# Two o matmuls moved by one place each in an attention and FFN kernel that TensorE bounds

## The chip, the cores and the metric

One core of a Trainium2 chip. The metric is the device time of one execution in microseconds (us), as a median over several executions; lower is better. Ratios are the mean time of one kernel's runs over that of the other's runs of the same rounds, so they are not quite the ratio of the medians that stand beside them. "Trace" is the profiler's record of one execution.

## The reference, cut to what matters

```python
B, H, S, Nb, D = 8, 8, 576, 16, 64
k_all = concat([beacon_k, k], axis=2); v_all = concat([beacon_v, v], axis=2)
scores = q @ k_all.T / sqrt(D)             # causal over the 576 keys, the 16 beacons always seen
a = softmax(scores); attn = a @ v_all
x = attn.transpose(0, 2, 1, 3).reshape(B * S, H * D)          # 4608 x 512
out = (gelu(x @ w_gate) * (x @ w_val)) @ w_out                # 512 -> 1536 -> 512
```

Eight batches of attention, then a gated FFN over all 4608 tokens. The kernel works in bf16 with float32 sums.

## The kernel before

The FFN works on chunks of 512 tokens, and each chunk's last product (the "o matmuls") is kept back: it is issued, a few matmuls at a time, inside the attention of the next batch, to fill TensorE while ScalarE computes exps. One step of the outer loop is thus: attention of batch b with 48 o matmuls of chunk b-1 strewn in (from batch 2 on, the first 12 are each split into two of 64 rows), then 96 gate and value matmuls ("gv").

Some words used below. A "burst" is a run of score matmuls, which read 64 rows each. "Values" is the product of the exps with v, by "head" or by "pair" of heads; it reads up to 128 rows. A "mode turn" is the place where TensorE goes from matmuls of 64 rows to matmuls of 128 or back. A "slot" is one of the three buffers of psum_s, where a burst's scores stay until ScalarE has computed their exps. "From start to start" is the time from the first matmul of a group to the first matmul of the next.

The helpers that matter (cut):

```python
psum_s = pool(name="psum_s", bufs=3, PSUM)   # 3 slots of two banks: scores, values pairs, gv
psum_t = pool(name="psum_t", bufs=1, PSUM)   # one bank
psum_o = pool(name="psum_o", bufs=1, PSUM)   # one bank

def scores(b, *parts):         # score matmuls on 64 rows, then one exp by ScalarE frees the slot
    s_ps = psum_s.tile(...)
    ...score matmuls of parts into s_ps...
    act(exp_ring[...], s_ps[...], ACT.Exp, scale=QK_SCALE)
    if b:
        ...masks(b, m, c): GpSimd affine_select on the diagonal blocks...

def av_head(b, m, hi, pool, tag):   # values of one head: 15 matmuls, then normalize (VectorE)
    x = pool.tile([P, 1, 512], FP32)
    attend(b, m, hi, x[:, 0, :])
    normalize(b, m, x, hi, hi + 1)  # reciprocal, then y_sb = x * r: frees the bank

def av(b, m):                       # both heads of a pair: 30 matmuls, in a psum_s slot
def out_mms(ci, u0, u1):            # o matmuls; every 12th starts a new bank, psum_t or psum_o
```

The stretch that the change touches, once for each of batches 1 to 7:

```python
            o(5 if b == 1 else 6)
            av_head(b, 0, 0, psum_t, "t")
            o(1)
            scores(b, (1, 1))           # third burst: three parts, 14 matmuls (10 in batch 1)
            scores(b, (2, 0))
            scores(b, (2, 2))
            ahead(2)                    # two loads for batch 2, in batch 1 alone
            av_head(b, 0, 1, psum_t, "t")
            turn_dma(b, 0)
            o(7)
            scores(b, (2, 1))           # fourth burst, 18 matmuls
            scores(b, (2, 3), (3, 3))
            scores(b, (3, 0))           # reuses the slot of (2, 2): waits for its exp
            av_head(b, 1, 0, psum_o, "o")
            o(5)
            av_head(b, 1, 1, psum_o, "o")
            turn_dma(b, 1)
            scores(b, (3, 1))
            scores(b, (3, 2))
            av(b, 2)                    # values pair 2
            turn_dma(b, 2)
            o(6)
            av(b, 3)                    # values pair 3: needs the masks of (3, 2)
            turn_dma(b, 3)
            o(11)
            ...gv matmuls of chunk b...
```

The softmax here doesn't subtract the row's maximum and nothing guards it: scores larger than these inputs give would overflow.

## Time and profile before

| | before |
|---|---|
| median of all 6 runs made beside the changed kernel | 365.87 us (365.26 to 366.03) |
| span of the traced execution | 363.7 us |
| TensorE busy | 98% of the span |
| attention stretch of batches 2 to 6, first o matmul to first gv matmul | 18.12 us each |
| the same of batch 1 and batch 7 | 19.11 and 18.17 us |

The kernel is one long chain on TensorE. In such a kernel the summed views (busy shares, waits) say only that little is left.

### The profile page before, as it was taken

The numbers are of one execution on the slowest core, as the hardware profiler recorded it, in microseconds if no ns is written. First come the engines' busy times: TensorE is split into PE (matmuls) and PEld (weight loads), VectorE is DVE, ScalarE is ACT, GpSimd is POOL, SyncE is SP. The second block draws the span as 40 slices with busy tenths as digits, with TensorE's granted clock in tenths as the row PEclk, the third lists the DMA queues.
The fourth block names the chain that finished last, engine by engine and source line by source line (L and its number), as shares of the span: only waits on it lengthen the run. The fifth ranks groups of instructions, "written<-read, shape, count | busy, mean of one in ns | idle before, by whom it ended". The sixth has DMA issues, their size and how long they took to land.

```text
span 363.7 us, 7774 instructions
## 1 busy us (share of the span) xinstructions
PE 356.0 (98%) x3206; PEld 186.8 (51%) x3206; DVE 163.0 (45%) x320; ACT 193.2 (53%) x252; POOL 161.2 (44%) x288
## 2 busy tenths in 40 slices
PE   7899999999999999999999999999999999999996
PEld 6665446444654455445644564446544564444443
DVE  4547846343543345434534354334443453333322
ACT  3965787238923693358633891379335953321210
POOL 8934397656536552845384645565320530000000
PEclk9999999999999999999999999999999999999999
DMA  8999999899179956999299917992795132000112
GB/s 105 175 203 204 197 125 109 122 175 182 28 122 146 214 46 83 155 212 69 56 151 213 116 38 124 171 192 30 116 139 128 17 68 108 0 2 29 58 38 108
DMA packets 160419, 41.57 MB, mean 114 GB/s; under 512 B 146944, under 2 KB 155904, under 8 KB 160384
## 3 DMA queue, kind: packets, MB, share of 16 engines
q0 software_dynamic: 104848, 19.11, 68.9%
q1 hardware_dynamic: 55536, 21.96, 30.3%
q8 instruction: 25, 0.41, 0.5%
q14 instruction: 10, 0.08, 0.1%
HBM read 38.27 MB, written 9.44 MB: 131 GB/s over the span
## 4 chain that ended last, share of the span: by engine, by line
PE 96%; DVE 3%; issue 0%; ACT 0%
PE gv_ps L168 45%; PE o_ps L168 26%; PE x_ps L168 9%; PE s_ps L168 6%; PE v_ps L168 3%; PE g_ps L168 3%; PE t_ps L176 2%; DVE qkT L235 1%; DVE o_sb L481 1%; PE w_ps L168 1%; PE y_ps L176 0%; ACT qkT L171 0%; DVE y_sb L356 0%; DVE o_sb L479 0%; DVE qkT L239 0%
## 5 line engine op out<-in xcount | busy, mean ns | idle before, releaser
L171 ACT ACTIVATE ge_sb<-gv_ps 128x512 bf16<-128x512 f32 x95 | 55.9, 597 | 135.3 <-PE gv_ps L168 134.1
L433 DVE TENSOR_TENSOR hT_sb<-gv_ps,ge_sb 128x512 bf16<-128x512 f32 x95 | 64.9, 691 | 105.4 <-ACT ge_sb L171 105.3
L171 ACT ACTIVATE expT<-s_ps 128x992 bf16<-128x992 f32 (+3 forms) x112 | 100.7, 974 | 11.3 <-PE s_ps L168 10.3
L168 PE MATMUL o_ps<-wo_sb,hT_sb 128*128 128x512 bf16 (+3 forms) x516 | 104.7, 373 | 0.9 <-DVE o_sb L481 0.9
L168 PE MATMUL gv_ps<-xT_sb,wg_sb 128*128 128x512 bf16 x380 | 105.4, 379 | 0.0
L168 PE MATMUL gv_ps<-xT_sb,wv_sb 128*128 128x512 bf16 x380 | 105.3, 379 | 0.0
L320 POOL TENSOR_SCALAR_AFFINE_SELECT expT<-expT 128x256 bf16<-128x256 bf16 (+1 forms) x140 | 52.3, 391 | 49.4 <-ACT expT L171 48.0
L168 PEld LDWEIGHTS <-wv_sb 128*128 128x128 bf16 x432 | 42.3, 98 | 50.6
L168 PEld LDWEIGHTS <-wg_sb 128*128 128x128 bf16 x432 | 42.1, 98 | 49.9
L168 PEld LDWEIGHTS <-hT_sb 128*128 128x128 bf16 (+1 forms) x516 | 40.8, 96 | 42.5 <-issue 4.1
L168 PEld LDWEIGHTS <-expT 128*128 128x128 bf16 (+1 forms) x960 | 33.6, 97 | 9.9 <-DVE y_sb L356 3.1
L168 PE MATMUL x_ps<-v_sb,expT 128*128 128x65 bf16 (+1 forms) x960 | 37.5, 193 | 0.1
L111 POOL DMA_DIRECT2D v_sb<-in_v_dram x40 | 33.6, 858 | 5.9 <-DMA wv_sb<-in_moe_w_val_dram 1.7
L168 PE MATMUL s_ps<-qkT 64*128 64x80 bf16 (+5 forms) x528 | 33.2, 250 | 2.4 <-DVE qkT L239 1.4
L111 POOL DMA_DIRECT2D k_sb<-in_k_dram x30 | 25.2, 844 | 16.7 <-DMA v_sb<-in_v_dram 8.2
L111 POOL DMA_DIRECT2D q_sb<-in_q_dram x30 | 25.3, 874 | 10.2 <-DMA wo_sb<-in_moe_w_out_dram 3.6
L356 DVE TENSOR_TENSOR y_sb<-x_ps,r_sb 128x320 bf16<-128x320 f32 (+1 forms) x47 | 28.8, 612 | 1.8 <-DVE r_sb L354 0.2
L479 DVE COPY o_sb<-o_ps 128x512 f32<-128x512 f32 (+2 forms) x31 | 20.7, 668 | 15.1 <-PE o_ps L168 14.2
L354 DVE RECIPROCAL r_sb<-x_ps 128x5 f32<-128x5 f32 (+1 forms) x47 | 9.6, 204 | 38.4 <-PE x_ps L168 38.4
L168 PEld LDWEIGHTS <-qkT 64*128 64x128 bf16 x528 | 18.7, 95 | 15.2 <-issue 7.0
L399 POOL COPY hold_sb<-xT_sb 128x2 bf16<-128x2 bf16 x6 | 1.1, 186 | 31.2 <-DMA xT_sb<-y_sb 31.2
L433 DVE TENSOR_TENSOR hT_sb<-v_ps,ge_sb 128x512 bf16<-128x512 f32 x13 | 9.0, 692 | 9.5 <-PE v_ps L168 9.5
(58 smaller groups left out, 151.6 us busy)
## 6 DMA issues: line engine op xcount, KB each, us to landing
out_dram<-o_sb SPq DMA_DIRECT2D x35, 256.0 KB, 7.2
v_sb<-in_v_dram POOLq DMA_DIRECT2D x24, 128.0 KB, 9.5
q_sb<-in_q_dram POOLq DMA_DIRECT2D x18, 128.0 KB, 12.6
k_sb<-in_k_dram POOLq DMA_DIRECT2D x18, 128.0 KB, 5.7
wo_sb<-in_moe_w_out_dram POOLq DMA_DIRECT2D x3, 512.0 KB, 14.4
wg_sb<-in_moe_w_gate_dram POOLq DMA_DIRECT2D x2, 512.0 KB, 11.3
wv_sb<-in_moe_w_val_dram POOLq DMA_DIRECT2D x2, 512.0 KB, 12.8
v_sb<-in_v_dram POOLq DMA_DIRECT2D x8, 112.0 KB, 5.7
```

The source lines that it names most:

```text
L111: keep(nc.gpsimd.dma_start(out=out_ap, in_=in_ap))
L168: keep(nc.tensor.matmul(out_ap, lhsT, rhs, start=start, stop=stop, **kw))
L171: keep(nc.scalar.activation(out_ap, in_ap, func, **kw))
L176: keep(nc.tensor.transpose(out_ap, in_ap, ident[0:n, 0:n]))
L235: keep(nc.vector.tensor_copy(out_ap, in_ap))
L320: nc.gpsimd.affine_select(out=d, in_=d, pattern=[[0, 2], [1, n]], compare_op=ALU.is_ge, fill=0.0, base=0, channel_multiplier=-1,)
L354: keep(nc.vector.reciprocal(r, x[:, :, :, D:DV]))
L356: nc.vector.tensor_tensor(out=y_of[i][:, :, h0:h1, :].rearrange("p j b d -> p b j d"), in0=x[:, :, :, 0:D], in1=r.to_broadcast([P, h1 - h0 ...
L399: keep(nc.gpsimd.tensor_copy(hold_sb, x[:, 0 : S : S - 1]))
L433: keep(nc.vector.tensor_tensor(out=h_of[ci][:, fi, :], in0=v_ps, in1=ge_sb, op=ALU.mult))
L479: keep(nc.vector.tensor_copy(o_ap, o_ps))
L481: keep(nc.vector.tensor_copy(o_ap, o_half))
```

## The change

Its intent, as the order tells it: start the exps of the third burst sooner, and give the last values pair more cover for its masks. No instruction is added or taken away, and only TensorE's order differs.

```diff
             av_head(b, 0, 0, psum_t, "t")
-            o(1)
             scores(b, (1, 1))
             scores(b, (2, 0))
             scores(b, (2, 2))
             ahead(2)
+            o(1)
             av_head(b, 0, 1, psum_t, "t")
 ...
             av(b, 2)
             turn_dma(b, 2)
-            o(6)
+            o(7)
             av(b, 3)
             turn_dma(b, 3)
-            o(11)
+            o(10)
```

Below, "part 1" is the first hunk and "part 2" the second.

## The prediction

> **What bounds the kernel now.** I read the page first (shares of the engines, then the chain that ended last), then who waited for whom, then the matmul timeline of single batches, because the change touches only a stretch of some 14 us in each of the seven later batches.
>
> ```profile
> PE 356.0 (98%) x3206; PEld 186.8 (51%) x3206; DVE 163.0 (45%) x320; ACT 193.2 (53%) x252; POOL 161.2 (44%) x288
> ...
> PE 96%; DVE 3%; issue 0%; ACT 0%
> ```
>
> TensorE (PE) is busy 98% of the span and makes up 96% of the chain that ended last. The other engines are half idle on average. No matmul is added or removed, so only bubbles between matmuls can be won. The three waits at issue, in sums over the whole run:
>
> ```profile
> ACT expT L171 <- PE s_ps L168: 10.3, 23, 1.0
> PEld L168 <- DVE y_sb L356: 4.6, 21, 0.3
> PEld L168 <- POOL expT L320: 0.8, 4, 0.2
> ```
>
> The first costs nothing directly (ScalarE is not the bound); the other two stop a weight load, and so TensorE. Most of the 4.6 us are not a full wait, as shown below. So the room is well under 2% of 365 us (7.3 us) before any detail.
>
> The detail: batch 3 between 128 and 142 us. First the third score burst (14 score matmuls), all engines, then the fourth burst and the last two values pairs on TensorE, and the same fourth burst in batch 7.
>
> ```profile
> 130.40 0.38 PE L168 MATMUL o_ps<-wo_sb,hT_sb 128*128 128x512 bf16 x1
> 130.71 0.81 PE L168 MATMUL s_ps<-qkT 64*128 64x80 bf16 x14
> 130.83 0.49 DVE L356 TENSOR_TENSOR y_sb<-x_ps,r_sb 128x320 bf16<-128x320 f32 x1
> 131.21 1.00 ACT L171 ACTIVATE expT<-s_ps 128x992 bf16<-128x992 f32 x1 [0.44 <-PE s_ps L168]
> 131.45 0.42 PE L168 MATMUL x_ps<-v_sb,expT 128*128 128x65 bf16 x8
> ```
>
> The o matmul starts at 130.40 and the scores at 130.71: 0.31 us, where a 512-column matmul in a stream takes 0.216 (eleven o matmuls took 2.37). So 0.10 us is a bubble at the turn from 128-row to 64-row matmuls; there is another of 0.09 at the turn back to x_ps. The exp of the burst waits 0.44 us for its scores. The second head (131.45) follows the normalize of the first (y_sb, done 131.32) by 0.13, so y_sb is just in time.
>
> ```profile
> 133.52 0.87 PE L168 MATMUL s_ps<-qkT 64*128 64x80 bf16 x18
> 134.33 0.62 PE L168 MATMUL x_ps<-v_sb,expT 128*128 128x65 bf16 x15
> ...
> 136.94 1.08 PE L168 MATMUL x_ps<-v_sb,expT 128*128 128x65 bf16 x30
> 137.87 1.46 PE L168 MATMUL o_ps<-wo_sb,hT_sb 128*128 128x512 bf16 x6
> 139.16 1.14 PE L168 MATMUL x_ps<-v_sb,expT 128*128 128x65 bf16 x30
> 140.14 2.54 PE L168 MATMUL o_ps<-wo_sb,hT_sb 128*128 128x512 bf16 x11
> ```
> ```profile
> 289.40 0.79 PE L168 MATMUL s_ps<-qkT 64*128 64x80 bf16 x18
> 290.13 0.63 PE L168 MATMUL x_ps<-v_sb,expT 128*128 128x65 bf16 x15
> ```
>
> From start to start, the fourth burst takes 0.81 us in batch 3 and 0.73 in batch 7. Inside the trace the difference is one gap of 69 ns, in batches 2 to 6, before its last score part: that part reuses the PSUM slot whose exp, the last of the third burst, ends at 133.95. In batch 7 TensorE happened to arrive later and did not wait. The same values work (30 matmuls) takes 0.93 us for pair 2 and 0.98 for pair 3: a gap of 57 to 58 ns behind the first matmul of pair 3, where its second weight load waits for the last mask of GpSimd (138.81 to 139.22).
>
> **What the Trainium skill says.** "TensorEngine Tiling (Array Packing)", Key Properties, says that a change of tiling mode drains TensorE. The trace agrees and prices it: 94 to 104 ns at each turn between 64-row scores and 128-row work, and none between x_ps and o_ps, which have 128 rows both. "Perfetto Trace Analysis", Optimization Strategy, advises to look for gaps on the limiting engine and for the semaphore behind each; that is the method here. "TensorE: Matmul & The Clock Gate", Back-to-back issue gap, gives N/2.4 + 2.5 ns, 216 ns for 512 columns, where sustained it quotes 131; this trace has 216 in long streams, so I use 0.216 us.
>
> **The change part by part.** The changed program, compared in the order of its instructions, differs on TensorE alone; the other four engines run the same list.
>
> Part 1, in batches 1 to 7: x(head 0), o, scores, x(head 1) becomes x, scores, o, x. Mode turns before: o to scores, scores to x. After: x to scores, scores to o. Two each, at 97 + 94 ns before and 100 + 94 after (x to scores takes 99 to 102 elsewhere in the batch): nothing, +3 ns. Head 1 begins at the same time, as the same work lies ahead of it. What moves is the scores: 0.31 - 0.10 = 0.21 us earlier. Then the exp starts 0.21 us earlier, since it had been idle for 0.44 us, and the two exps that follow it back to back also end 0.21 us earlier, the last at 133.74 in place of 133.95. The fourth burst then finds its slot free (it would need it at 133.93): the 69 ns go, in five batches (2 to 6): 5 x 0.069 = 0.35 us. In batch 7 there is none to win; its 0.14 us wait for a late y_sb ahead of head 1 stays, for VectorE's list is the same and the o matmul that moves was inside that wait's shadow before as after.
>
> Does the earlier burst meet a wait of its own? Its last part needs the exp that ends at 130.76 (batch 3). It would start at 131.16 - 0.22 = 130.94: free, by 0.13 us with the semaphore's 0.04. Batch 7 likewise. In batch 1 not: there ScalarE is behind, and the exp ends at 53.13 while the part would start at 52.99. It loses 0.20 us there:
>
> ```profile
> 52.18 0.95 ACT L171 ACTIVATE expT<-s_ps 128x928 bf16<-128x928 f32 x1
> ...
> 52.76 0.80 PE L168 MATMUL s_ps<-qkT 64*128 64x80 bf16 x10
> ...
> 58.92 1.30 PE L168 MATMUL x_ps<-v_sb,expT 128*128 128x65 bf16 x30
> 60.06 1.46 PE L168 MATMUL o_ps<-wo_sb,hT_sb 128*128 128x512 bf16 x6
> ```
>
> But pair 2 of batch 1 takes 1.14 us where it takes 0.93 in batch 3: it waits 0.205 us for masks that GpSimd does late, between its own DMA issues. A delay of 0.20 is swallowed there. Batch 1 comes out at 0, give or take 0.1.
>
> Part 2, in batches 1 to 7: one o matmul moves from behind the last pair to ahead of it. 0.216 us of work now lies where 58 ns were lost, so the mask is in time. Batches 2 to 7: 6 x 0.058 = 0.35 us; batch 1 shows no such gap. The transposing DMA of the last pair leaves 0.216 - 0.058 - 0.07 = 0.09 us later, while the FFN of the chunk starts 0.127 earlier. It takes 2.6 us to land after its issue at 141.70, so 144.3; the first matmul that reads it is the thirteenth of the FFN stream, 142.52 + 12 x 0.216 = 145.1. The 0.8 us of slack shrink to 0.6: no new wait.
>
> Sum: 0.35 + 0.35 + 0 = 0.70 us less, 0.19%. 365.3 - 0.7 = 364.6 us.
>
> **The rivals.** (a) The burst waits in more batches than the first: it is 0.13 us from doing so, and a wait there is a loss of TensorE with the o matmul stuck behind it in order. If all of 2 to 7 lost 0.1 us, 0.6 us would go and the result would be 365.2. Against it: the exps of batches 2 to 7 lie within 0.02 us of each other in the trace. (b) Batch 1's 0.20 us isn't swallowed, because with ScalarE later the masks come later too: 364.8. (c) y_sb turns into the bound ahead of head 1: it is done 0.08 us before it is needed, and it does not move; but a weight load that could run under the o matmul is held up a little: at most 0.02 us x 7. (d) ScalarE's lead is worth more than I count and removes gaps elsewhere: I found no other gap that is not a mode turn or TensorE's own y_sb wait, so at most 0.3 us more. (e) Nothing happens, because the gaps only move on to the FFN: there the gv stream shows no gap after the first matmul, so what is won before it is kept.
>
> **Range and chances.** The terms are small against the runs' scatter: the three of before go from 365.26 to 365.93. I take 364.6 with 363.9 to 365.4: below, d and scatter; above, a plus b. 2% would be 7.3 us, ten times all that I can find, and no dependence changes that could cost that much: faster 0.01, same 0.98, slower 0.01.
>
> **What would show it.** Fourth burst of batches 2 to 6 at 0.74 us from start to start; pair 3 at 0.92 to 0.93 in all batches; ScalarE's wait ahead of the third burst's exp down from 0.44 to about 0.22; third burst of batch 1 longer by 0.2 and its pair 2 shorter by as much; head 1 starting as long after head 0 as now; no gap in the FFN streams. It is wrong if the third burst waits for exps in batches 2 to 7, if pair 3 still has its gap, or if the span does not fall by the sum of the closed gaps.

## The result, and the profile after

The changed kernel takes 364.71 us (median of 6, 364.54 to 365.37) where the kernel before takes 365.87 (median of 6, 365.26 to 366.03). The ratio is 0.9975, with a 95% interval from 0.9963 to 0.9988: 0.25% faster, clear of noise and inside the 2% that counts as the same. The predicted 364.6 us is 0.1 off; how much of that is luck is told below.

The page of the changed kernel, its engines:

```profile
PE 353.7 (97%) x3164; PEld 187.5 (52%) x3206; DVE 163.4 (45%) x320; ACT 193.0 (53%) x252; POOL 161.3 (44%) x288
```

The 2.3 us that TensorE seems to have lost are no gain. 42 of 3206 matmul records are missing from this trace (the weight loads are all there): 24 o matmuls and 18 gv matmuls. The traces of the first four experiments lack 42 too; the other six traces lack none. In the stretches below, the o matmul that is missing is the first behind a values group: from start to start such a values group has some 0.22 us in it that belong to an o matmul not shown, and the next o group has a count one too small. This is to be kept in mind in the timelines.

TensorE in batch 3 of the changed kernel (columns: start in us, length in us, engine, line, operation, out<-in, shape, count):

```profile
130.29 0.62 PE L168 MATMUL x_ps<-v_sb,expT 128*128 128x65 bf16 x15
130.84 0.80 PE L168 MATMUL s_ps<-qkT 64*128 64x80 bf16 x14
131.58 0.39 PE L168 MATMUL o_ps<-wo_sb,hT_sb 128*128 128x512 bf16 x1
131.81 0.61 PE L168 MATMUL x_ps<-v_sb,expT 128*128 128x65 bf16 x15
...
133.87 0.79 PE L168 MATMUL s_ps<-qkT 64*128 64x80 bf16 x18
134.59 0.62 PE L168 MATMUL x_ps<-v_sb,expT 128*128 128x65 bf16 x15
...
139.64 1.07 PE L168 MATMUL x_ps<-v_sb,expT 128*128 128x65 bf16 x30
140.55 2.32 PE L168 MATMUL o_ps<-wo_sb,hT_sb 128*128 128x512 bf16 x10
```

ScalarE's exp behind the third burst there:

```profile
131.34 1.00 ACT L171 ACTIVATE expT<-s_ps 128x992 bf16<-128x992 f32 x1 [0.22 <-PE s_ps L168]
```

From head 0 (130.29) to head 1 (131.81) it is 1.52 us, as before (129.94 to 131.45, 1.51). The exp waits 0.22 us in place of 0.44. The fourth burst takes 0.72 us from start to start in place of 0.81, and pair 3 takes 0.91 in place of 0.98 (its missing record lies behind pair 2 here, so this group is whole).

Batch 6 of the changed kernel shows what the prediction had not seen:

```profile
247.19 0.97 PE L168 MATMUL s_ps<-qkT 64*128 64x80 bf16 x14
248.09 0.39 PE L168 MATMUL o_ps<-wo_sb,hT_sb 128*128 128x512 bf16 x1
```

Here the third burst takes 0.91 us from start to start, in batch 3 only 0.74. The table has the attention stretch of each batch, from the start of its first o matmul to the start of its first gv matmul, in us, read from the matmul starts of each trace. Between these stretches the FFN is the same to 1 ns. So the difference of two kernels is known from single traces to some 10 ns in batches 2 to 5 and some 20 ns in batches 6 and 7 (batch 7 has 18.105 to 18.126 us in the four traces that have both parts there and no padding), which the medians of the times can't give: they carry the start of the program, which took from 21.3 to 23.6 us up to the first FFN matmul in the eleven traces.

| batch | before | after | part 1 alone | part 2 alone | fourth burst later | after, padded |
|---|---|---|---|---|---|---|
| 1 | 19.106 | 19.104 | 19.118 | 19.120 | 19.191 | 19.471 |
| 2 | 18.122 | 17.969 | 18.032 | 18.056 | 18.033 | 17.963 |
| 3 | 18.120 | 17.962 | 18.027 | 18.049 | 18.033 | 17.961 |
| 4 | 18.121 | 17.966 | 18.029 | 18.054 | 18.037 | 17.967 |
| 5 | 18.120 | 17.965 | 18.033 | 18.049 | 18.031 | 17.968 |
| 6 | 18.121 | 18.137 | 18.195 | 18.053 | 18.037 | 17.965 |
| 7 | 18.174 | 18.109 | 18.172 | 18.121 | 18.171 | 17.964 |
| sum less before | | -0.672 | -0.278 | -0.382 | -0.351 | -0.625 |

The sum after is -0.67 us where -0.70 was predicted. But it is made of four batches with -0.15 to -0.16, one with +0.02 (batch 6), one with -0.065 and one with nothing. The two traced spans hardly differ (363.7 and 363.6 us), because the changed kernel's traced execution began its first FFN matmul 0.50 us later (22.38 against 21.88); its fastest runs have a span of 362.8.

### The profile page after: what moved, and what is told of

Its sections match the earlier page's. It is cut to its first block, busy times and chain, and to the rows that moved or that the text cites. A ratio compares the mean times of both kernels' runs of the same rounds, so it can differ in the third digit from the quotient of the medians.

```text
span 363.6 us, 7732 instructions
## 1 busy us (share of the span) xinstructions
PE 353.7 (97%) x3164; PEld 187.5 (52%) x3206; DVE 163.4 (45%) x320; ACT 193.0 (53%) x252; POOL 161.3 (44%) x288
## 4 chain that ended last, share of the span: by engine, by line
PE 88%; DMA 5%; DVE 3%; POOL 2%; issue 1%; ACT 0%; SPq 0%; POOLq 0%
PE gv_ps L168 40%; PE o_ps L168 25%; PE x_ps L168 9%; PE s_ps L168 6%; DMA q_sb<-in_q_dram 3%; PE v_ps L168 3%; PE g_ps L168 3%; PE t_ps L176 2%; DMA k_sb<-in_k_dram 1%; DVE qkT L235 1%; POOL v_sb L111 1%; PE w_ps L168 1%; DVE o_sb L481 1%; DMA xT_sb<-y_sb 1%; POOL k_sb L111 0%
## 5 line engine op out<-in xcount | busy, mean ns | idle before, releaser
L168 PE MATMUL o_ps<-wo_sb,hT_sb 128*128 128x512 bf16 (+3 forms) x492 | 101.0, 373 | 2.3 <-DVE o_sb L481 0.9
L168 PE MATMUL gv_ps<-xT_sb,wv_sb 128*128 128x512 bf16 x364 | 101.7, 379 | 0.4
```

The source lines that it names most:

```text
L168: keep(nc.tensor.matmul(out_ap, lhsT, rhs, start=start, stop=stop, **kw))
```

## The experiments

All outputs are right. The first four ran in one call, on one chip, with 11 runs of the kernel before (median 365.66 us; two of them took 368.0 and 368.3, so these intervals are wide); the next four in another (365.92 us); the last as one look. Each was timed with six runs, the last with one.

**Part 1 alone.** Is the gain of the fourth burst due to the earlier exp, and what does the early burst cost?

```diff
 (the first hunk of the change; the last pair as before)
```

> Part 1 alone (third burst right behind the first head), last pair as before. My theory: the fourth burst of batches 2 to 6 falls from 0.805 us to 0.72 (its slot wait goes), pair 3 keeps its 0.98, the third burst is held for 0.17 us in batch 6 and 0.2 in batch 1 (swallowed by pair 2 there). By attention stretch against before: batches 2 to 5 about -0.09 us each, 6 about +0.08, 7 and 1 about 0; in all -0.3 us. Rival (the whole gain is part 2's, the fourth burst gets shorter only because all before it moved): fourth burst stays at 0.805, total 0.

Measured: 365.47 us, ratio 0.9977 (0.9948 to 1.0007), too wide for the times to tell. TensorE in batch 3:

```profile
133.97 0.79 PE L168 MATMUL s_ps<-qkT 64*128 64x80 bf16 x18
134.69 0.62 PE L168 MATMUL x_ps<-v_sb,expT 128*128 128x65 bf16 x15
...
139.52 1.14 PE L168 MATMUL x_ps<-v_sb,expT 128*128 128x65 bf16 x30
140.50 2.54 PE L168 MATMUL o_ps<-wo_sb,hT_sb 128*128 128x512 bf16 x11
```

The fourth burst is at 0.72, pair 3 keeps its 0.98. The stretches fell by 0.09 us in batches 2 to 5, and batch 6 grew by 0.07, as my theory had it. The rival (all of it is part 2's) falls: part 2 was not in this kernel.

**Part 2 alone.** The wait of the last pair.

```diff
 (the second hunk of the change; the single o matmul ahead of the third burst as before)
```

> Part 2 alone (one more o matmul ahead of the last values pair). My theory: pair 3 falls from 0.98 to 0.912 us in batches 2 to 7, fourth burst stays at 0.805, third burst as before: 6 x -0.068 = -0.4 us. Rival (the mask comes later by as much, the wait only moves): pair 3 stays at 0.98, total 0.

Measured: 365.35 us, ratio 0.9982 (0.9951 to 1.0012). In batch 3:

```profile
135.19 0.87 PE L168 MATMUL s_ps<-qkT 64*128 64x80 bf16 x18
135.99 0.62 PE L168 MATMUL x_ps<-v_sb,expT 128*128 128x65 bf16 x15
...
141.04 1.07 PE L168 MATMUL x_ps<-v_sb,expT 128*128 128x65 bf16 x30
141.95 2.32 PE L168 MATMUL o_ps<-wo_sb,hT_sb 128*128 128x512 bf16 x10
```

Now it is the other way round: the fourth burst stays at 0.80, pair 3 falls to 0.91. Six batches lose 0.053 to 0.071 us each. The two parts together, -0.278 and -0.382, make -0.660, and the whole change has -0.672: they add up, and neither feeds the other.

**Fourth burst later.** If its gap is a wait for the slot that the last exp of the third burst frees, more time must close it as well as an earlier exp does.

```diff
             turn_dma(b, 0)
-            o(7)
+            o(8)
             scores(b, (2, 1))
 ...
             turn_dma(b, 3)
-            o(11)
+            o(10)
```

> Before, with one o matmul moved from the end of the stretch to ahead of the fourth burst; third burst and last pair untouched. If the 83 ns of the fourth burst are a wait for the PSUM slot that the third burst's last exp frees, giving it 0.216 us more time closes them without any earlier exp: fourth burst 0.72 us in batches 2 to 6, in all -0.4 us, and the third burst of batch 6 not held. If the gap has another cause (order of parts, a bank), it stays at 0.805 and the total is 0.

Measured: 365.36 us, ratio 0.9974 (0.9942 to 1.0006). In batch 3:

```profile
134.01 0.79 PE L168 MATMUL s_ps<-qkT 64*128 64x80 bf16 x18
134.74 0.62 PE L168 MATMUL x_ps<-v_sb,expT 128*128 128x65 bf16 x15
```

The burst takes 0.72 us with the third burst where it was, and 0.084 to 0.089 us go in batches 2 to 6, batch 6 among them, whose third burst is not held. So what the gap needs is time, as a wait for that slot would, and not an earlier exp in itself. This move closes it without the cost that part 1 has in batch 6: without batch 1 (see below) its stretches sum to -0.436 us, those of part 1 alone to -0.290. It was not run together with part 2.

**The changed kernel, padded.** Why is batch 6 different? Its exp ahead of the third burst is late in both kernels, before and after alike. ScalarE in batch 6 of the kernel before, then of the changed kernel:

```profile
245.23 1.78 ACT L171 ACTIVATE expT<-s_ps 128x832 bf16<-128x832 f32 x2 [0.36 <-PE s_ps L168]
```
```profile
245.12 1.78 ACT L171 ACTIVATE expT<-s_ps 128x832 bf16<-128x832 f32 x2 [0.36 <-PE s_ps L168]
```

In other batches this exp follows the one before it within 0.08 us, and measured from the exp before it is 0.28 us earlier than here. The view puts the 0.36 us down to the score matmuls, but by their records those of this exp had ended 0.38 us before it began (in batch 3, 0.10 us). VectorE shows the like once, at a y_sb of batch 7, 0.24 us behind its reciprocal where 0.03 is usual:

```profile
286.68 0.49 DVE L356 TENSOR_TENSOR y_sb<-x_ps,r_sb 128x320 bf16<-128x320 f32 x1 [0.24 <-DVE r_sb L354]
```

Both are the 320th traced instruction of their engine, with the waiting and issuing ones, which a page doesn't count as busy, counted in. So the test adds a few tiny instructions ("padding") to both engines long before, in the FFN of batch 0 (fi counts its 12 steps).

```diff
+            if b == 0 and fi in (3, 5, 7, 8, 9):          # in the FFN of batch 0
+                for _ in range(2):
+                    act(act_pad, idle[:, 0:2], ACT.Copy)
+            if b == 0 and fi in (2, 3, 5, 7, 9, 10):
+                for _ in range(2):
+                    keep(nc.vector.tensor_copy(dve_pad, idle[:, 0:2]))
```

> The changed kernel with 10 tiny ScalarE and 12 tiny VectorE instructions added to the first batch's FFN, where both engines idle; results unchanged. In both kernels the 320th traced instruction of ScalarE (an exp of batch 6) and of VectorE (a y_sb of batch 7) starts late by 0.28 and 0.21 us with nothing to wait for, and a packet on the queue of instruction loads follows each by about 1 us. If that is tied to the count of instructions, both lags move into the FFN: batch 6 third burst back from 0.906 to 0.737 us, batch 7 o matmul ahead of head 1 from 0.358 to 0.227, in all -0.3 us against the changed kernel. If they are tied to the place or to traffic at that time (rival), both stay and the total is 0 against the changed kernel.

Measured: 364.87 us, ratio to the kernel before 0.9962 (0.9933 to 0.9990). The third burst of batch 6, then that of batch 7, in this kernel:

```profile
247.07 0.80 PE L168 MATMUL s_ps<-qkT 64*128 64x80 bf16 x14
247.81 0.39 PE L168 MATMUL o_ps<-wo_sb,hT_sb 128*128 128x512 bf16 x1
...
286.59 0.39 PE L168 MATMUL o_ps<-wo_sb,hT_sb 128*128 128x512 bf16 x1
286.81 0.61 PE L168 MATMUL x_ps<-v_sb,expT 128*128 128x65 bf16 x15
```

The burst of batch 6 is back at 0.74 us, and the o matmul ahead of head 1 in batch 7 at 0.22 (0.36 in the changed kernel). Batches 6 and 7 took 0.172 and 0.145 us less than in the changed kernel, and all of batches 2 to 7 now take 17.96 to 17.97. So the lags do not belong to the place in the work. Batch 1, though, took 0.367 us more: its first values head waited for GpSimd.

```profile
52.02 0.44 PE L168 MATMUL x_ps<-v_sb,expT 128*128 128x65 bf16 x9
52.89 0.36 PE L168 MATMUL x_ps<-v_sb,expT 128*128 128x65 bf16 x6 [0.44 <-POOL expT L320]
```

GpSimd computes the masks in order with the loads that it issues for batch 2. In this trace two such issues, 1.62 us, stood ahead of masks where the changed kernel's trace had 0.75 us between 47.9 and 48.7. The same wait, shorter, is in the traces of "fourth burst later" and, below, of "two o matmuls ahead of the last pair" and "batch 1 alone", none of them padded, and not in the padded one of "all of it"; so it comes and goes between traces, and batch 1 is no measure for any variant.

**Guard for batches 1 and 6.**

```diff
             av_head(b, 0, 0, psum_t, "t")
+            if b in (1, 6):
+                o(1)
             scores(b, (1, 1))
             scores(b, (2, 0))
             scores(b, (2, 2))
             ahead(2)
-            o(1)
+            if b not in (1, 6):
+                o(1)
             av_head(b, 0, 1, psum_t, "t")
```

> The changed kernel, but batches 1 and 6 keep the old place of the single o matmul (ahead of the third burst). Theory: in these two the early burst only runs into an exp that is late, so batch 6's third burst falls back from 0.906 to 0.737 us while its fourth burst keeps 0.72 (its arrival is late anyhow) or returns to 0.805; batch 6 gains 0.09 to 0.17 us against the changed kernel. Batch 1: third burst 0.73 in place of 0.95, and the wait of pair 2 for its masks opens again by about 0.2, so nothing in sum. Rival (the order costs batch 1 its 0.2 us for good): batch 1 gets shorter by 0.2.

Measured: 364.94 us, ratio to before 0.9978 (0.9964 to 0.9991). Batch 6 takes 18.053 us, 0.084 less than in the changed kernel: the third burst is at 0.74 again, but the fourth is back at 0.81 from start to start, so only the lower end of what I expected was there. Batch 1: third burst 0.73, pair 2 wait open again (1.13 us for its 30 matmuls), 19.103 us in sum, the same as after (19.104) and before (19.106). So the early burst's 0.2 us in batch 1 are swallowed by waits behind it, as predicted.

**Two o matmuls ahead of the last pair.**

```diff
-            o(7)
+            o(8)
             av(b, 3)
             turn_dma(b, 3)
-            o(10)
+            o(9)
```

> The changed kernel with two more o matmuls ahead of the last pair in place of one (8 ahead, 9 behind). The wait that was there is 68 ns and one matmul of 216 ns covers it, so the second brings nothing: pair 3 at 0.912 us, 0.0 us against the changed kernel. Rival (the last pair's transposing transfer then lands too late for the FFN): a gap at the thirteenth matmul of the FFN, up to 0.1 us a batch; I expect none, as some 0.4 us of slack are left.

Measured: 365.10 us, ratio to before 0.9982 (0.9965 to 0.9999). The stretches are those of the changed kernel within 0.017 us, pair 3 at 0.91, and the FFN behind has no gap. One matmul of 0.216 us covered the wait; the second buys nothing and costs nothing.

**Batch 1 alone.** One of the o matmuls goes where batch 1 really waits, ahead of pair 2.

```diff
+            if b == 1:
+                o(1)            # ahead of the third burst, as before; b > 1: behind it
             ...
+            if b == 1:
+                o(1)
             av(b, 2)
             turn_dma(b, 2)
-            o(7)
+            o(6 if b == 1 else 7)
```

> The changed kernel, but in batch 1 the single o matmul stays ahead of the third burst, and one of the seven o matmuls between the last two pairs goes ahead of pair 2, whose masks are late there. Theory: the 0.2 us wait of batch 1 is covered by 0.216 us of work; batch 1's attention stretch about 0.2 us shorter than in the changed kernel, unless the masks of pair 3 are late in turn. The rest as in the changed kernel. Total -0.2 us, small beside the scatter of the start.

Measured: 365.10 us, ratio to before 0.9980 (0.9966 to 0.9993). Not shown by this trace as a whole: batch 1 took 19.293 us, 0.189 more than in the changed kernel, for its first head waited 0.39 us for masks, as above. The wait that was aimed at is gone (pair 2 at 0.91 us).

**All of it.** Padding, batch 1 order, and the change.

> The changed kernel with the batch 1 order of the run before and the padding that moves the late 320th instruction of ScalarE and VectorE into the FFN. Batch 1 -0.2 us (if its v load is not what it waits for), batch 6 -0.17, batch 7 -0.14 against the changed kernel: 0.3 to 0.5 us less than it, near 364.2 us if the changed kernel is at 364.7; the batch lengths will say it more exactly than the times.

Measured: 364.37 us (six runs, 364.13 to 365.39), ratio to before 0.9962 (0.9948 to 0.9976). In this trace batch 1's first head had its masks in time, and the o matmul ahead of pair 2 shows its worth:

```profile
60.06 0.39 PE L168 MATMUL o_ps<-wo_sb,hT_sb 128*128 128x512 bf16 x1
60.29 1.07 PE L168 MATMUL x_ps<-v_sb,expT 128*128 128x65 bf16 x30
61.20 1.03 PE L168 MATMUL o_ps<-wo_sb,hT_sb 128*128 128x512 bf16 x4
```

Batch 1 takes 18.892 us, 0.212 less than in the changed kernel, batch 6 0.172 less, batch 7 0.146 less. The seven stretches sum to 1.20 us less than before, where the change has 0.67. It is the fastest version by stretches and by median. It was run at another time. Its interval overlaps that of the changed kernel, so that it beats the changed kernel rests on the stretches.

**A smaller padding.** Is it the 320th instruction?

```diff
 (the changed kernel with 3 ScalarE and 2 VectorE tiny instructions at fi == 3 of batch 0)
```

> The changed kernel with 3 tiny ScalarE and 2 tiny VectorE instructions added in the first batch's FFN. If the lag belongs to the 320th traced instruction of an engine, the late ones are now what were the 317th of ScalarE (the exp two before, of batch 6) and the 318th of VectorE (the reciprocal of batch 7's first head), each some 0.2 to 0.28 us later than in other batches, and the old 320ths are no longer late by themselves; batch 6 and 7 then lose about as much as in the changed kernel, because the late exp still delays those behind it and the late reciprocal still delays head 1. Rival (padding of any kind cures it, or the lag is tied to place or traffic): the same instructions as before are late, or none.

Measured, one look: 365.07 us against 366.02 for the kernel before. I was wrong in part. Batches 6 and 7 are cured (17.965 and 17.964 us), and neither of the new 320th instructions is late in a way that shows. But batch 4, which had been clean in every other run, takes 18.332 us, 0.366 more. VectorE, then TensorE, at the end of the FFN ahead of batch 4:

```profile
162.61 0.69 DVE L435 TENSOR_TENSOR hT_sb<-v_ps,ge_sb 128x512 bf16<-128x512 f32 x1 [1.34 <-PE v_ps L168]
163.84 0.69 DVE L435 TENSOR_TENSOR hT_sb<-v_ps,ge_sb 128x512 bf16<-128x512 f32 x1 [0.54 <-PE v_ps L168]
```
```profile
163.75 0.58 PE L168 MATMUL s_ps<-qkT 64*128 64x512 bf16 x6
164.59 0.39 PE L168 MATMUL s_ps<-qkT 64*128 64x80 bf16 x8 [0.26 <-DVE hT_sb L435]
```

The second product of VectorE starts 0.46 us after the matmul it waits for had ended, and a score burst that needs its slot waits for it. It is VectorE's 192nd traced instruction, 128 ahead of the 320th. So with two padding instructions on VectorE a lag of the same kind stood in another batch, in the one trace that there is. That the lags depend on how many instructions stand ahead, and not on the work at their place, stands: the two of batches 6 and 7 are in all eight traces without padding and in none of the three with it. That they fall on each 128th, or which instruction near it is hit, is not shown: the new 320ths were not late.

## Why the prediction was right, point by point

**Fourth burst** (predicted 5 x 0.069 = 0.35 us). Mechanism right, shown twice, by an earlier exp (part 1 alone) and by more time (fourth burst later). The size was 0.083 us a batch: I had counted only the one gap of 69 ns; the mode turn behind the waiting burst also gave back 8 ns (from the last score matmul to the first values matmul it is 318 ns before and 310 after), and the last few are spread over the burst.

**Last pair** (predicted 6 x 0.058 = 0.35 us). Mechanism right, shown by part 2 alone. The size was 0.068 in batches 2 to 6, pair 3 going from 0.980 to 0.912 us, and 0.382 us in all. I had counted one gap of 58 ns; the other 10 ns are spread over the group.

**Third burst, mode turns and head 1** (predicted nothing). In batch 3 head 1 comes as long after head 0 as before, 1.52 and 1.51 us. Right, but for batch 6 (rival a). The prediction has y_sb done 0.13 us ahead of head 1 in one place and 0.08 in another; nothing rests on which.

**Batch 1** (predicted nothing, give or take 0.1). The held burst was there (0.95 us in place of 0.73), and so was the swallowing: 19.104 against 19.106 us. Pair 2 gave back 0.18 us of it and the fourth burst, which the prediction had not counted here, 0.035.

**Rival a failed as I had judged it.** The prediction said that the exps of batches 2 to 7 lie within 0.02 us of each other. I had read batches 3 and 7. Batch 6 is 0.28 us late in the very trace I predicted from, and its third burst was held for 0.17 us, which cost all that batch 6 had to gain: +0.016 us where -0.127 was predicted. This step was wrong, and by the prediction's own sign too ("it is wrong if the third burst waits for exps in batches 2 to 7"). That the sum came out close is luck: the two sizes were 0.12 us too small (5 x 0.083 and 6 x 0.068 are 0.82), and the held burst took 0.17 back.

**Where the sums end.** Predicted -0.70, stretches -0.67, medians -1.16, ratio 0.9975 of 365.87, which is -0.91 with -0.44 to -1.35 as its interval. The times agree with the stretches, but could not have told -0.67 from -1.2. That the time itself was met within 0.1 us is luck as well: the prediction started from 365.3 us, the middle of three runs of the kernel before, and six of them have 365.87.

**What stays open.** Why a single instruction starts late with nothing to wait for. Loading of instructions is a suspect: in both traces a packet of 8192 bytes on the queue of instructions follows the late exp by 0.9 to 1.0 us and the late y_sb by 0.7 to 0.9 us. In the padded runs the packets moved, but not by the same rule (behind the late product of the smaller padding the next one comes only after 2.3 us), and no run takes the loading away.

## What to carry to other kernels

In a kernel that TensorE bounds to 98%, a reordering is worth the sum of the bubbles it closes, no more; list them by start-to-start times in every repetition, not in two of them, because the repetition that differs is the one in which the new order runs into something. Where a bubble is a wait for a slot, as in the fourth burst here, moving filler work ahead of the waiting group did as much as advancing the producer, and didn't bring a new group closer to its own waits. When times scatter by 1 us, compare stretches between two landmarks of the traces.

## What the Trainium skill lacked or had wrong

- "TensorEngine Tiling (Array Packing)", Key Properties, says that a change of tiling mode drains TensorE, without a price. Here each turn between 64-row and 128-row matmuls without another wait cost some 92 to 103 ns in the trace of the kernel before (start to start, less 216/512 ns for each column; the prediction reads 94 to 104).
- "TensorE: Matmul & The Clock Gate", Back-to-back issue gap, quotes about 131 ns for each 512-column matmul in a sustained stream with weight loads. Here it was 216 ns in every long stream (eleven o matmuls in 2.37 us), as its own formula for a single gap has it.
- "Runtime: NRT & Kernel Launch", Instruction fetch mechanics, calls the cost of crossing a block of 256 instructions mostly hidden. Whether that is the cause here is open, but no page tells of single ScalarE and VectorE instructions that start 0.2 to 0.5 us late and move when a few instructions are added ahead: with two padding instructions on VectorE, one trace shows batch 4 0.37 us longer. The instruction packets seen beside them were of 8192 bytes (those of the other instruction queue are of 16384).
- No page says that a trace can lack matmul records alone, with their weight loads there. Here 42 of 3206 were missing in five of the eleven traces, and each looks like a gap of 0.22 us in the timeline.
